# Summing the attention denominators on GpSimd in place of VectorE, in a linear-attention and MLP kernel on one core

## The chip, the cores and the metric

The kernel runs on one NeuronCore of a Trainium2 chip. The metric is the time of one execution on the device in microseconds (us), as the median of several runs. TensorE multiplies matrices, VectorE and ScalarE work elementwise and along rows, GpSimd here does reductions over partitions, and SyncE (SP) issues the transfers, one after the other in its own queue. All engines run side by side and each works its own queue in order; what has to wait for another engine waits on a semaphore.

## The reference

```python
batch, n_heads, seq, head_dim = (8, 8, 576, 64)      # d_feat = 128
def phi(x):
    proj = np.einsum('bhsd,df->bhsf', x, w_phi)
    proj = proj - np.max(np.abs(proj), axis=-1, keepdims=True)
    return np.concatenate([np.exp(proj), np.exp(-proj)], axis=-1)
q_p, k_p = (phi(q), phi(k))
kv = np.einsum('bhsf,bhsd->bhfd', k_p, v)
z = np.sum(k_p, axis=2)
num = np.einsum('bhsf,bhfd->bhsd', q_p, kv)
den = np.einsum('bhsf,bhf->bhs', q_p, z)[..., None] + 1e-06
attn = num / den
...
x = attn.transpose(0, 2, 1, 3).reshape(B * S, H * D)   # 4608 x 512
r = np.maximum(x @ w_in, 0.0)                          # d_ff = 2048
return (r * r) @ w_out
```

For each of 64 heads, a feature map of 2 x 128 exponentials is made of the queries and of the keys; `kv` and `z` collect the keys, `num` and `den` apply them to each query, and the quotient goes through a two-layer network with a squared ReLU. The change is about how `den` is formed: one number for each of the 576 queries of a head, a sum over 256 features.

## The kernel before

The 64 heads are worked in 32 pairs. A pair's tokens are 576 columns; the two heads of a pair lie on the partitions, 64 dimensions each, or 128 features each. Four pairs make a batch element, 576 tokens. The network runs over 18 chunks of 256 tokens, each in 8 blocks of 256 hidden columns: `gemm1` (24 products, line L1164), a squared ReLU on ScalarE and VectorE that yields a high part `gh` and a low part `gl`, then `gemm2` (L1195). The last four chunks take another form of the second product (L1440). A chunk can start as soon as the tokens of its pairs lie in a ring of buffers (`ring`, written by `tokens`, L937 to L959).

All of this is interleaved. Every piece of work is entered by `P.add(engine, us, function, after, buffers, rank, ...)`; a planner (`Plan.order`) runs through it like a clock, with a cost in us for each piece, one free time for each engine and the buffers that a piece holds, and takes on each engine the ready piece of the lowest rank. The order that comes out is the order of the instructions on each engine. The ranks of most pieces come from a string, `RANKS`, two characters each:

```python
op.rank = (90 * i + j - 3000) * 0.05
```

The argument `lock` stands for a resource that VectorE and GpSimd share in the planner: a GpSimd piece with a lock waits for the end of a VectorE piece with one, and such a VectorE piece is lengthened by what is left of a GpSimd piece, up to `lock` us.

Pairs 0 to 5 (`early`) run beside the loading and splitting of the weights. They form their denominators on TensorE, and `denominators` (L917) adds 1e-6, takes the reciprocal on a tile `den` of 128 x 9 (L919, L920), writes it to DRAM (`rd`), and `spread` reads it back onto all partitions (`rb`).

Pairs 6 to 31 (`visit` and `late`) go like this. In `late`, TensorE projects the queries with the features on the partitions (L1065), the result is copied to `pt` (L320, L322), GpSimd takes the maximum over partitions of each head (`partition_all_reduce`, L1088), VectorE subtracts it, ScalarE takes the two exponentials (L1093, L1095), and ScalarE and VectorE weigh them with `z` into y, which stands in `pt` (L1100, L1102): the denominators are then the sums of y over 128 partitions. VectorE forms them in steps: it transposes 32 x 32 blocks into `yt` (L1106), sums along the rows into `d4` (L1107), SP takes the result through DRAM (`dd`, then `da`) so that the four blocks of partitions come side by side, and VectorE adds them, adds 1e-6, takes the reciprocal and transposes back (`inverse`, L1117 to L1120). Two transfers write it to `rd`, and `spread` follows. `yt` has one buffer, which the sums of `z` use too (L1041, L1043); `pt` has one buffer. `narrow` (L655 on) splits queries and keys into halves with a scale that GpSimd finds by small maxima (L664).

Of the kernel before, what the change touches and what calls it, by code (L numbers as in the profile page):

```python
# [301 lines left out]
def tile_kernel(ctx, tc, qp, kp, vp, w_phi, w_in, w_out, out):  # L302
# [332 lines left out]
    def narrow_weights(rank):  # L635
# [4 lines left out]
            wk[1], wk[0], channels=128, reduce_op=bass_isa.ReduceOp.max), [o, pool_next], [], rank, lock=0.0)  # L640
# [395 lines left out]
    def late(p):  # L1036
# [48 lines left out]
        for h in range(2):  # L1085
# [20 lines left out]
            o = P.add("DVE", dve_us(S), lambda n=n, y=y: V.transpose(yt_["y", n - 2 * EARLY], y()), [o], [("pt", p), ("yt", ("y", n - 2 * EARLY))], R(RQ + 0.9))  # L1106
            dens.append(P.add("DVE", dve_us(S), lambda n=n, h=h: V.tensor_reduce(  # L1107
                out=d4_[p][:, h, :], in_=yt_["y", n - 2 * EARLY].rearrange("p (b x) -> p b x", x=32), op=ALU.add, axis=AX.X),
                [o], [("yt", ("y", n - 2 * EARLY)), ("d4", p)], R(RQ + 1.0)))
# [3 lines left out]
        o = P.add("SP", 0.4, lambda: SP.dma_start(da_[p], dd_[p].rearrange("(a x) y -> x a y", a=4)), [o],  # L1113
                  [("dd", p), ("da", p)], R(RQ + 1.1), land=1.9, xfer=0.1)

        def inverse():
            V.tensor_reduce(out=dr_[p][:, 0:36], in_=da_[p].rearrange("p a x -> p x a"), op=ALU.add, axis=AX.X)  # L1117
            V.tensor_scalar(out=dr_[p][:, 0:36], in0=dr_[p][:, 0:36], scalar1=1e-6, scalar2=None, op0=ALU.add)
            V.reciprocal(out=dq[:, :, 0:18], in_=dr_[p].rearrange("p (h x) -> p h x", h=2))
            V.transpose(dt_[p], flat(dq))  # L1120
# [4 lines left out]
        def keep():
            for h in range(2):
                SP.dma_start(rd_[p].rearrange("(h x) y -> h (x y)", h=2)[h].rearrange("(b x) -> b x", x=32),
                             dt_[p][0:18, 32 * h:32 * h + 32])
# [113 lines left out]
    def norm(src, after, rank, j, i):  # L1242

        keys = [("j", j)], [("n1", i)], [("n2", i)]
        box = lambda: j_.at(j, [128, KT, T], BF16)
# [3 lines left out]
        o = P.add("POOL", par_us(T), lambda: G.partition_all_reduce(  # L1249
            n2_[i], n1_[i], channels=128, reduce_op=bass_isa.ReduceOp.add), [o, pool_next], keys[1] + keys[2], rank, lock=0.0)  # L1250
# [318 lines left out]
    "W.if#M#F8n#L,_6.89$W/E#z--$l%x.;+i+3%z)G$5&E$V$5(j+(!|1E*y5U$L#L&V#L-111(q?,$7.m#=WxK*4.NmoDAw>*-t,E"
    "G.`$D-WD!G*(HfMKRnkkJ!&iLH&w,rS49g0+EzH5LC%Y!GK3U=1A*3a)*D1PJW1iEcopphh5T,]$_[(aQp!_$*&dK*H)6g1IvchL"  # L1570
    "-{Ty#ksC[8iCv!e[0[?lQl3G8{5^N0Ba(bT9ix,CV2leVy`0($Q8pp8!/ZdsrKQ`PERPxl#|<g(pt*3J#<3%2}xly!e^R&ynpSyW"
    "uFu.q]gkzPL;QYzQq4(5xTn`zJ2(v*Mb]iOh|b?YgwR_n-KIj5RZxPhV[sadjQW|W*oRk8wVdmA3y?o*tJ}M{TPG>.:EX-PXL6,T"
    "ClMR*t_[X41`LUI1dZ|xaV}/{?<|z-t^lRi*v6i[mW|Vz=|X}+e)r7Ax`+K,DVC,FK*/;9vj=}nQA7M6*;Vl}i^c27s$K$5pVS5P"
# [79 lines left out]
```

## Time and profile before

| | us |
|---|---|
| median of 3 runs | 1032.64 |
| lowest and highest run | 1032.29, 1034.31 |
| profiled execution | 1029.46 |
| its span, first to last instruction | 1027.7 |
| TensorE matmul busy | 994.9 |
| VectorE busy | 824.1 |
| ScalarE busy | 740.5 |
| GpSimd busy | 169.1 |

The profile is one execution. In its rows, PE is TensorE's matmuls, PEld its weight loads, DVE VectorE, ACT ScalarE, POOL GpSimd and SPq the queue of SP. A row of a group gives line, engine, operation, the tile written and the tiles read, shapes and count, then busy us and the mean in ns, then the idle time before it and what ended that. A row of a tile or a line gives the count, the shortest, median and longest duration in ns, and the first and last start in us. A row of waits says who waited for whom: us in total, times, the longest. A row of the table by stages gives the stage, its length, and for PE, PEld, DVE, ACT and POOL the busy us and the number of instructions, then the granted clock of TensorE, the share of the DMA engines and GB/s. A row of the timeline gives start, duration and what ran.

### The profile page before, as it was taken

The numbers are of one execution on the slowest core, as the hardware profiler recorded it, in microseconds if no ns is written. First come the engines' busy times: TensorE is split into PE (matmuls) and PEld (weight loads), VectorE is DVE, ScalarE is ACT, GpSimd is POOL, SyncE is SP. The second block draws the span as 40 slices with busy tenths as digits, with TensorE's granted clock in tenths as the row PEclk, the third lists the DMA queues.
The fourth block names the chain that finished last, engine by engine and source line by source line (L and its number), as shares of the span: only waits on it lengthen the run. The fifth ranks groups of instructions, "written<-read, shape, count | busy, mean of one in ns | idle before, by whom it ended". The sixth has DMA issues, their size and how long they took to land. (4 is left out here: it accounts for less than half of the span.)

```text
span 1027.7 us, 21125 instructions
## 1 busy us (share of the span) xinstructions
PE 994.9 (97%) x8247; PEld 717.0 (70%) x8310; DVE 824.1 (80%) x1547; ACT 740.5 (72%) x1346; POOL 169.1 (16%) x100
## 2 busy tenths in 40 slices
...
DMA packets 92936, 76.28 MB, mean 74 GB/s; under 512 B 61476, under 2 KB 70308, under 8 KB 90788
## 3 DMA queue, kind: packets, MB, share of 16 engines
...
## 5 line engine op out<-in xcount | busy, mean ns | idle before, releaser
L1164 PE MATMUL ph<-ring,win 128*128 128x256 f16 x3456 | 391.8, 273 | 1.4 <-DVE gl L315 1.4
L1164 PEld LDWEIGHTS <-win 128*128 128x128 f16 x3456 | 336.0, 98 | 58.5 <-issue 9.8
L1088 POOL PARTITION_ALL_REDUCE mx<-pt x52 | 116.0, 2232 | 497.7 <-ACT pt L320 196.9
L1195 PE MATMUL po<-wh,gh 128*128 128x512 f32 x456 | 146.0, 441 | 0.0
L1195 PE MATMUL po<-wl,gl 128*128 128x512 bf16 x455 | 118.2, 382 | 0.1
L1176 ACT ACTIVATE r<-ph,cw 128x512 f32<-128x512 f32 x114 | 77.6, 681 | 55.5 <-PE ph L1164 55.1
L1195 PE MATMUL po<-wl,gh 128*128 128x512 bf16 x394 | 107.0, 379 | 5.9 <-issue 3.5
L315 DVE TENSOR_TENSOR gl<-ph,gh 128x512 bf16<-128x512 f32 x114 | 77.3, 678 | 34.9 <-ACT ph L1180 31.3
L1195 PEld LDWEIGHTS po<-wh,gh 128*128 128x128 f32 x456 | 86.1, 189 | 26.2
L1195 PEld LDWEIGHTS <-gh 128*128 128x128 bf16 x456 | 42.0, 98 | 49.1 <-issue 8.2
L1195 PEld LDWEIGHTS <-gl 128*128 128x128 bf16 x456 | 35.3, 98 | 58.3 <-issue 26.7
L1178 ACT ACTIVATE gh<-r 128x512 fp32r<-128x512 f32 x114 | 71.1, 624 | 3.7 <-PE po L1195 1.5
L1180 ACT ACTIVATE ph<-r 128x512 f32<-128x512 f32 x114 | 67.0, 588 | 0.4
L768 PE MATMUL pv<-e,v 128*64 128x256 f32 x512 | 62.8, 389 | 3.2 <-ACT kz L322 2.0
L315 DVE TENSOR_TENSOR qe<-pt,mx 128x576 f32<-128x576 f32 x52 | 39.0, 751 | 20.2 <-POOL mx L1088 18.7
L315 DVE TENSOR_TENSOR v<-qe,gh 128x896 f16<-128x896 f32 x30 | 32.6, 1089 | 27.2 <-ACT gh L1428 27.0
L1093 ACT ACTIVATE qe<-qe 128x576 f32<-128x576 f32 x52 | 35.2, 677 | 20.1 <-DVE qe L315 19.8
L1102 DVE SCALAR_TENSOR_TENSOR pt<-qe,zc,pt 128x576 f32<-128x576 f32 x52 | 42.1, 809 | 9.5 <-ACT pt L1100 9.2
L768 PEld LDWEIGHTS pv<-e,v 128*64 128x64 f32 x512 | 35.0, 141 | 20.7 <-ACT kz L322 2.9
L1413 ACT ACTIVATE r<-ph,cwr 128x512 f32<-128x512 f32 x30 | 20.6, 686 | 34.2 <-PE ph L1164 34.0
L1440 PEld LDWEIGHTS <-gh 128*128 128x128 f16 x420 | 41.1, 98 | 4.8
L1249 POOL PARTITION_ALL_REDUCE n<-n x12 | 22.2, 1848 | 119.3 <-DVE n L1247 79.7
...
## 6 DMA issues: line engine op xcount, KB each, us to landing
...
kz<-td SPq DMA_DIRECT2D x104, 32.0 KB
zq<-zd SPq DMA_DIRECT2D x104, 2.0 KB
```

What stands on the lines that cost most here:

```text
L315: eng.tensor_tensor(out=out_, in0=a, in1=b_, op=ALU.subtract)
L768: PE.matmul(out=to[64 * h:64 * h + 64, 0:256], lhsT=v_[p][:, t, h, :], rhs=e_[2 * p + h][:, t].rearrange("p s f -> p (s f)"), start=t == 0 ...
L1088: o = P.add("POOL", par_us(S), lambda n=n, h=h: G.partition_all_reduce(mx_[n], pt_[p][:, h, :], channels=128, reduce_op=bass_isa.ReduceOp. ...
L1093: o = P.add("ACT", act_us(S), lambda qe=qe: A.activation(out=qe(1), in_=qe(0), func=AF.Exp, scale=-1.0), [o], [("qe", n)], R(RQ + 0.4))
L1102: o = P.add("DVE", dve_us(S), lambda h=h, qe=qe, y=y: V.scalar_tensor_tensor(out=y(), in0=qe(1), scalar=zc_[p][:, 2 * h + 1:2 * h + 2], in ...
L1164: PE.matmul(out=ph[:, j, :], lhsT=win[w][:, t, 128 * ff:128 * ff + 128], rhs=ring[half][x][:, t, c0:c0 + T], start=k == 0, stop=k == 3 * K ...
L1176: o = P.add("ACT", act_us(512, 1), lambda: A.activation(out=r_[n], in_=ph_[bank], func=AF.Relu, scale=cw[:, f, 0:1]), [g1], [("ph", bank), ...
L1178: sq = P.add("ACT", act_us(512), lambda: A.activation(out=gh_[n], in_=r_[n], func=AF.Square), [o], [("r", n), ("gh", n)], Q)
L1180: o = P.add("ACT", 0.59, lambda: A.activation(out=ph_[bank], in_=r_[n], func=AF.Square), [o], [("ph", bank), ("r", n)], Q, other=("DVE", 0 ...
L1195: PE.matmul(out=po_[po[i][1]], lhsT=g[:, j, 128 * i:128 * i + 128], rhs=w[:, j, :], start=(f == (NFP - ENDS if last else 0) and (s, j) == ...
L1249: o = P.add("POOL", par_us(T), lambda: G.partition_all_reduce(n2_[i], n1_[i], channels=128, reduce_op=bass_isa.ReduceOp.add), [o, pool_nex ...
L1440: PE.matmul(out=to, lhsT=l()[:, a], rhs=r(slice(b_, b_ + 1))[:, 0], start=(f == 0 and k == 0 and place % 2 == 0), stop=(f == NFP - 1 - END ...
```

## The change

In `late`, the transposition, the row sums, the two transfers through DRAM and the long `inverse` go. In their place GpSimd sums y over partitions for each head, by `partition_all_reduce` with `add`, into `yt`; one transfer for each head takes one row of the result into the 128 x 9 tile `den`, and the `denominators` function that pairs 0 to 5 use does the rest. All `partition_all_reduce` pieces, old and new, are entered with `lock=None`, so the planner no longer counts them for the shared resource. The tiles of the old steps go, and the string of ranks is another one, with two pieces fewer for each of the 26 pairs.

```diff
-    dd_ = tiles(dr, "dd", [128, 36], F32, 2, EARLY)
-    d4_ = tiles(sm, "d4", [128, 2, 18], F32, 1, EARLY)
-    da_ = tiles(sm, "da", [32, 4, 36], F32, 1, EARLY)
-    dr_ = tiles(sm, "dr", [32, 36], F32, 1, EARLY)
-    dt_ = tiles(sm, "dt", [32, 64], F32, 1, EARLY)
...
-    dq = cp.tile([32, 2, 32], F32, name="dq")
...
-    V.memset(dq, 0.0)
...
             o = P.add("POOL", par_us(S), lambda n=n, h=h: G.partition_all_reduce(
                 mx_[n], pt_[p][:, h, :], channels=128, reduce_op=bass_isa.ReduceOp.absmax),
-                [pt[0], pt[1 + h], pool_next], [("pt", p), ("mx", n)], R(RQ + 0.2), lock=0.0)
+                [pt[0], pt[1 + h], pool_next], [("pt", p), ("mx", n)], R(RQ + 0.2), lock=None)
...
-            o = P.add("DVE", dve_us(S), lambda n=n, y=y: V.transpose(yt_["y", n - 2 * EARLY], y()), [o], [("pt", p), ("yt", ("y", n - 2 * EARLY))], R(RQ + 0.9))
-            dens.append(P.add("DVE", dve_us(S), lambda n=n, h=h: V.tensor_reduce(
-                out=d4_[p][:, h, :], in_=yt_["y", n - 2 * EARLY].rearrange("p (b x) -> p b x", x=32), op=ALU.add, axis=AX.X),
-                [o], [("yt", ("y", n - 2 * EARLY)), ("d4", p)], R(RQ + 1.0)))
-
-        o = P.add("SP", 0.4, lambda: SP.dma_start(dd_[p], flat(d4_[p])), dens, [("d4", p), ("dd", p)], R(RQ + 1.1),
-                  land=1.9, xfer=0.1)
-        o = P.add("SP", 0.4, lambda: SP.dma_start(da_[p], dd_[p].rearrange("(a x) y -> x a y", a=4)), [o],
-                  [("dd", p), ("da", p)], R(RQ + 1.1), land=1.9, xfer=0.1)
-
-        def inverse():
-            V.tensor_reduce(out=dr_[p][:, 0:36], in_=da_[p].rearrange("p a x -> p x a"), op=ALU.add, axis=AX.X)
-            V.tensor_scalar(out=dr_[p][:, 0:36], in0=dr_[p][:, 0:36], scalar1=1e-6, scalar2=None, op0=ALU.add)
-            V.reciprocal(out=dq[:, :, 0:18], in_=dr_[p].rearrange("p (h x) -> p h x", h=2))
-            V.transpose(dt_[p], flat(dq))
...
-        o = P.add("DVE", 0.95, inverse, [o], use, R(RQ + 1.1), lock=4.0)
...
-        o = P.add("SP", 0.7, keep, [o], [("dt", p), ("rd", p)], R(RQ + 1.1), land=1.9, xfer=0.1)
...
+            key = [("yt", ("y", n))]
+            o = P.add("POOL", 3.56, lambda n=n, y=y: G.partition_all_reduce(
+                yt_["y", n], y(), channels=128, reduce_op=bass_isa.ReduceOp.add), [o], [("pt", p)] + key,
+                R(RQ + 0.9), lock=None)
+            dens.append(P.add("SP", 0.5, lambda n=n, h=h: SP.dma_start(
+                den_[p][64 * h:64 * h + 64], yt_["y", n][0:1].rearrange("j (r x) -> j r x", x=9)), [o],
+                [("den", p)] + key, R(RQ + 1.0), land=2.1, xfer=0.1))
+
+        denominators(p, dens, lambda h: rd_[p].rearrange("(h c r) x -> h c (r x)", c=2, h=2)[h].unsqueeze(0).to_broadcast(
+            [64, 2, SH]), R(RQ + 1.1))
...
-    "2{E!VZ&L$^O6(*5%-iV(D=6%E}8(1QS^iie/I`Tah!BjSAa18U7u838rvqGxgEVBwm84DII)w9[Xrvy!LR.sT%|Eg=vlGX{6mA0E"
...
+    "C^D[FxBfEXD^D6F*DhCDI3DGGEEEG`I@GWH?GUH-FBHEGxH>HNHNG{HGEuIoFnM)HXHNGjH(GsGtHKI1DVISFvI<HXIJJ)HnIEHd"
...
```

More of the change, by code (lines that the diff above doesn't have):

```diff
@@ L639, in narrow_weights @@
         o = P.add("POOL", par_us(1), lambda: G.partition_all_reduce(
[L640 removed]
+            wk[1], wk[0], channels=128, reduce_op=bass_isa.ReduceOp.max), [o, pool_next], [], rank, lock=None)
         def bits():
@@ L664, in bound @@
             G.partition_all_reduce(x[:, 0:2], ka_[p], channels=128, reduce_op=bass_isa.ReduceOp.max)
-        o = P.add("POOL", par_us(2), bound, last + [pool_next], uses[:2], rank + 0.1, lock=0.0)
+        o = P.add("POOL", par_us(2), bound, last + [pool_next], uses[:2], rank + 0.1, lock=None)
         def bits():
@@ L1122, in late @@
-        use = [("da", p), ("dr", p), ("dt", p)]
-        o = P.add("DVE", 0.95, inverse, [o], use, R(RQ + 1.1), lock=4.0)
[L1125 to L1128, printed above, removed]
-        o = P.add("SP", 0.7, keep, [o], [("dt", p), ("rd", p)], R(RQ + 1.1), land=1.9, xfer=0.1)
-        spread(p, o, lambda h: rd_[p].rearrange("(h c r) x -> h c (r x)", c=2, h=2)[h].unsqueeze(0).to_broadcast([64, 2, SH]),
-               R(RQ + 1.1))
+            key = [("yt", ("y", n))]
@@ L1249, in norm @@
         o = P.add("POOL", par_us(T), lambda: G.partition_all_reduce(
-            n2_[i], n1_[i], channels=128, reduce_op=bass_isa.ReduceOp.add), [o, pool_next], keys[1] + keys[2], rank, lock=0.0)
+            n2_[i], n1_[i], channels=128, reduce_op=bass_isa.ReduceOp.add), [o, pool_next], keys[1] + keys[2], rank, lock=None)
         return o, i, keys[2]
@@ L1274, in split_norms @@
         o = P.add("POOL", par_us(NFP), lambda: G.partition_all_reduce(
-            wt[:, NFP:], wt[:, 0:NFP], channels=128, reduce_op=bass_isa.ReduceOp.max), rows + [pool_next], [], rank + 5.0, lock=0.0)
+            wt[:, NFP:], wt[:, 0:NFP], channels=128, reduce_op=bass_isa.ReduceOp.max), rows + [pool_next], [], rank + 5.0, lock=None)
         def bits():
@@ L1569 @@
[L1569 to L1573, printed above, removed]
@@ new lines @@
+    "HkIRHdH0HtH}JWIPILH|HaJ;I>I-ITJ6HoM9K(E@IBEyL7FTICHxERK=P4INI#IAI7J3EVHZM%JZI#J%JoHWJ,K%JGJhJgJfLrEG"
+    "K5N&L$KKMIL%J_L%LWLSOgNULLN*H,ItJ$PLK@IYN(K}KlInJAJEGrJAJ2IVIMR(Q&I}GeQOJyPrQ;O/ChM^O!GgMxP#I>N}O%PB"
+    "NqN8RzNzBvCHD$DJD,?GD{MnDRCsD;D#CADMDKC^DYDcDiAJD`DbCzD,D}D.D2D;D4DTCQDNDmDcD0F3D&F/HHF0DrC[F>G7HRE6"
+    "CaB/CxDIDSDaE>E<DxDjE=HdBcE8F[?HG_G*FMD;E+F2GpEcC<E!GcE(E^EqE;HOF%I)E`E^DaB2BOBWAbCA@|HxC7D^Cl?`BVAB"
+    "EkByBPBbBPBL@(BiBF;FAaDVC$@}AHE*;JF)C{Ee?IA|Bb?QC4E!@&B{BLB=AM@bBv@WBOITFQG^EYG|FeGmJ)G%G7G?KXK`>wB4"
@@ new lines @@
+    "EDG?FdG%FbF%GOG7G:DZG^GVGsE|GTIJFhGfFMH[<XGdHrFeG9FyG6E<GEC0F>L2H9J9E!J=I$H]HOH_F;D^K0D@FXErGkH=H_J5"
+    "H]BaN&H@I9I^J4GgErGiH8JXI!I&H$GNF0I$F5I>HGEjK{KJGtLnF*JzI1JbIJCNIOJ!I-HBHtMNI:IHJ)EgJ=KzG7FVIfJUH^K5"
+    "FmG]I/IqIdJ$HoH&HJIrJ2J1DyMNJgJoL|NNFnJZP-GsG3F!J7J/ImI#IyIyM%I3I.I6K%I6E:IOJZJYJNIrGeK^KXL.KBOVNtJI"
+    "L;McL=LlMYI,J%MKGUITIHKcMBC|GWIRJZJYJBHDJKJKM=KTK>K$@,JEJ$J`J*JYJyMpK[I^M)IXJxK[LMF,P.IbL8PfKqO+HyKZ"
+    "KLS7I1FHLHHJJ)I}J<JpKzLSM!KTMrMXKOP}LHP!L!GPGjK|NZKuQtSyN6N0JhGhOBHvFQO?QHCxK/K4OeHyKpK.PPDDLoFhJiHL"
@@ new lines @@
+    "LGOpRDJYG5CyNhF[NlR&JgN/GVM+FRI6MyM3JLG^MRKvGvKZNrE?QjJAKZO`AXD)K6VnIzIRN1GmNXQ*CwMyT_LlNrO?R5N|M<G2"
+    "R!S!G!JYM&O]FYOnJ(OdO_JiS-UpTGRfJRH[QZTzQWPGOiRBPnQQUvRLLDKAMdR,McO{L?F=N3MtJcKLPCU2Q;JGO$J8P|OOMv]2"
+    "MeL$JPKKT8KOK8RtJlN4NCPFK[O,RzPTNNT!QpL!NcQEQZUcOgO:QVRIOoO7LuQ{OJPYRDR{NlSGPbPvPqWGR^P_NSR=T<M9PZSV"
+    "TyR9M1O1T1TiT`PG`!PlO]LUT]ORSdMzY:O=Q!KUPZM*RyP@Q/PIQ4OjPoQ!Q=PGPWL%ImTeDFPIPkOaNnO3SCQMNUSIHfPOS!SE"
+    "OsT)P&O0NoOHH@N#JeNhQ6IWMTLCTHNpP6W5R(LNOBN.SDMQM2VuREPXOuN=TORNQ!ODPsIGL@N-Q`O/JUQjQRPKREQ.NKTMQXLr"
@@ new lines @@
+    "K4KuOqKZQhT;PkPuWVT9Q(RbOWO]MELjN{QAQ[SnN&RoOANZPLN#S.M2MWPRQ+UHLwRAS9OxKEN?KtPNOeOAUmPCRRQWP0SURFLi"
+    "S*QHL%NAQDN;JuO;L{Q(O=UBPmTtPoNxQTTdQkUTX)T-W4UoUBP2Q)StSpQwQ%PyTJQ>R8SOOvR#ShQSSIQ+PuR8UrQOWaN}PGK#"
+    "R1SiNqafYFUrWjWdZ^UJQ-Y5K}X7P7OTKKR>WPLoO.VUS=TLRGR9UFTjR:UFUsRoRQYTSrOMMrHwKpMzLcPEK>MuPxJ;M6IhOtQ["
+    "KnPTHBI]IaS$QCODP^NzN`JjPVOMAsNJJpL9Q/P0PdNALTP6QUV|TTNdNZG$LNVmLbQIN^O_U)O|QOJ/P5PWOfJ3N_Q:JKLlO:Th"
+    "VBXmT=UfQ,UkJoTFTzWNR6RVOLV&UCP7W0NmPvU6RLSmRLT,VyW8PsRhRAOxLCO[Q=S4R.V+U}K{T{VRZ3R}Uf^9X=Pj^EPqWiV."
@@ new lines @@
+    "U1Z^P`XKVkRaR>SaSbRoRrT!]1`jOUQRTnR9T6RVQyRXM@Q(RWSZR#S?Q6V]L]R*SRR&QVU]R9QFT%QoQ>ONSPYrT&SqP>P0UBSg"
+    "R*PoPjNpSPMyTGQ6U!M/K@MkS7SpR6QiWES)QIP}QlYqQKS(V{WfWmY;[*Y;WX_aN@S%Q-T;R1TLUFS{S}R`WQZEX[`4]v]pZYXy"
+    "W3V^]CX`S7].VT^)Yn_VYIVrUQXYX,XzVJWRY-SmXXTLY-U}SD[[X|]qV,UGV5_z`D^jW8b9X9V(Q.Y0YkWn_[b2^lYiYuZXXla%"
+    "`h_8a+^BXVYo]oV[U1THT5XRWiTmYkKwUXVIS]U/R)`[U1U9V^Z/W.W:W.VmW|V&QlX#YYXwV&_QX6W{];XuXSU0VQTZX%X[YsTT"
+    "ZSWoS,POXpXtZQUe[fW2YVXtWfXZWfZ1WpXKZ!XMX8Y3VhVhWWXvXtZSU=YDS3V@W#V_V,TfTXWoW!YuSXUiZBYKX(Z;UOXoW+]0"
@@ new lines @@
+    "ZIQ_Y-Z^Ws`*Zj`_UXWOX=Vk]xWLWUZ*UyV,[$RV]eW8]+].Y8f?[lX)_T[pZeW3`)U`UeXnX_ToU]T6XuWBTrVyXeTiVZWOYjV>"
+    "XvW0ZLV0XdXTWuUuW_X-ZLU3Y=V+XZY@RjP9ZSS+Y2We[i[eVyXyVVXKRvU}YaWrS7S]Z-W-VDR}XCXBS^UGRu_<X+ShYYYCYgXb"
+    "VF[&ZfZ9W!W7X-UjUPXuU7W?S>XxZ5VjWg[k[>Y]PwY&]R[tY/ZWZxWxYX[QWP_E^BY$_MZyZ2^2ZZ]ZX3]4[kXdVnZ6Yg]Z[)]g"
+    "W8Z$VAY][4ZdYl]A]GRq]{Yw]oYhW$dj[1Zs_vZQYr[D]2W|[zZ=^#]DZ7UpWFTuXUZH]hU_Z,ZfUwZvYK]0]dXN^>YUWbY{Ut[+"
+    "Y@X8XHX!ZYU&Z,V2WQZgQWScY?QKZ8VmZcX(Ys[)VeY,V_OQXUUOWOWfXKX:VtYhbk^6Z4[sTnV]Y4YfY5_KU?]k^`X1ZkUuS;X]"
@@ new lines @@
+    "SbYGX._+Z8^hY>ZANZSpW4Q|R)W7S_ZBW2_i^$[UbfW]V7RU[0Mh[RXVS1YB[>c_W>Q3W%N3TTW=bNU[X)^=O(UeUXV$W|X&V?a7"
+    "XtV&U.ZXSwVyUgXX_yWJRHZrUPVS_E]A`&[}YrVYbGYyWz[Z`t[=^!Z6^jYoc8[-`{^bXCU[[HY_SIWK^]]>Y:[XVx[)`p^vZ>dt"
+    "^y[__([cfw`.[]aucmZ>X{`xeFe-d|YMfHcEg`ZZV`VmZ-]waxfhYAX}YK^oZu^2Xn]D`qSoZI_&Y0awZ&^OZdadXvg3^5Z6U>aV"
+    "YA_9]LV4[6ULYbX5a-XiT}Xac/U|X+d=ZvZ^daTic7Y{Yec/]`_b]U^pdVZ5`YUtX<T6bigQfN_c`wT$Y7[LZNc.^]d|^<T&XH_q"
+    "dx[C`^es^k]hXPZx_#[rZoWnZ`V<bt]QZ_[QZ&WHWC_:_z]R`FcY^4]f]2]+X?`!al`V^w_t[i_jc0a+]R[eW![!^V[ObF_a[yZp"
@@ new lines @@
+    "^MZh_^cpaa][X{aO[VY}VJ_!b=^1YYWQU{^N^r_Nf>d&`k_/]$`z_.[cZ_a+]F^V`k`*]=^]a]_T`we/^Q`tfEb1a;d?a``?^ZiC"
+    "]o_)bW_X`P_t]t`*`h`Gcvd@e$b1^e_pbB_l^edxcjehak`_^h]xgxaVcEa)Y_ZH^s__b<cCb%exfVbFbS`W_F_TcbckaUa<_ZZE"
+    "]`^2_Xa^c]cHdb`FcggTfSZ;`]d3aT]R_1[YbX[Zece^cOdS]e[<b{bEbTcHfcg0YchjcqXpcsf6hz`8Xob-aQfzoGdPdZ^=]J[x"
+    "aAYodrb}lNc<_5mbc/c;`vbH`lVmc^et_TboYScx[]dUapb5`$aFd7e,`@^>`M]p`ia_c9^BdEc%ah_-bvfH`;fUd*[6`t`,c:a="
+    "`_dx`c^ler]-ZncNgu_J_?cU_x_r[kdHa[fya}ZV_jedesd^ckiNddbs^P_r^F`?_vaVcJbNgi[7dTbZcx[pb$abaY^/bC`?cC]W"
@@ new lines @@
+    "d+avbhbo`eaIn4dea[a.a%_:bia#b+a7gv_yd)a{c>_0fYdgdsZ#au^YZRh!].c-d/`J`Ba=[Qa[f1bcfkaD`cd.c*hZ`ob%c%e:"
+    "b@e<a`gTdVb;f@bzc^iEbVb^bqe-ae^gb<cdbQb2ayeDeIa._Ze8e4bBdjbcf^c^`#c^b-g)c2ece}hOas_d_>eeeidnb/g<cqm6"
+    "_gbmcPkaamj.dCg}cHc|bQa(^^b7c]a?[!X!^{fma;di]4aXg^guitba_ldY_/jGf`g8jP`{`ddtb?cwaJj<iDe3dMg:d@]KhGdL"
+    "elem^UWy]@fta/eWYdZ4ag`*ZiZ4_8`s[u]y]{fL^e`$_KUJaV[n^g`K_-`Fa8^8al[la)aNe4[>ZMZc]e`z_vd._;FwRiOQL@K="
+    "NyVoR-TuQzMtOeO#Q&NyR-PST]Q*M_QtP9RHX&R_VWPaPQG[QFNqPON8L7L_UCElS+SoSoV2[FS:VJTkRYOuQ[PHIMP%PTP#ViT("
```

57 lines of the change are left out of this document (8 added, 49 removed).

## The prediction

> **What bounds the kernel now.** I read the page's totals first, then the table by stages, then the waits of TensorE in the two parts that the table separates.
>
> ```profile
> span 1027.7 us, 21125 instructions
> PE 994.9 (97%) x8247; PEld 717.0 (70%) x8310; DVE 824.1 (80%) x1547; ACT 740.5 (72%) x1346; POOL 169.1 (16%) x100
> ...
> 0.00:125.00 125.00, 103.19 (x1068) 71.43 (x1071) 108.27 (x173) 108.61 (x189) 17.55 (x12) 0.97 0.58 208
> 125.00:875.00 750.00, 742.98 (x5845) 514.37 (x5905) 626.66 (x1200) 553.34 (x1022) 147.92 (x86) 1.00 0.25 64
> ```
>
> The span is 1027.7 us and the profiled execution took 1029.46, so 1.76 lie around the span. The median of the runs is 1032.64: 3.2 above the profiled execution. I sum against 1029.46 and add 3.2 at the end.
>
> The stage table is the argument. Of 1027.7 - 994.9 = 32.8 idle us of TensorE, 125.0 - 103.19 = 21.8 lie in the first stage, 750.0 - 742.98 = 7.0 in the long middle and so 4.0 after it. Pairs 6 to 31 live in the middle: their first GpSimd maximum starts at 145.4 us and their last at 829.1 (row below). So the change is made in the stage where TensorE has 7 us to give back, and VectorE, although 84% busy there (626.66 of 750), is not what TensorE waits for:
>
> ```profile
> PE po L1195 <- issue: 3.5, 22, 0.2
> PE pn L418 <- ACT pt L322: 0.8, 1, 0.8
> PE pp L1065 <- DVE e L731: 0.3, 1, 0.3
> PE po L1195 <- ACT r L1176: 0.2, 1, 0.2
> ...
> PE po L703 <- DMA k<-in_kp_dram: 4.4, 1, 4.4
> ```
>
> The first four lines are all the waits of TensorE from 125 us on: 3.5 us is its own issue, and only 0.3 us of the 4.8 was spent behind VectorE. The last is the longest of the first 125 us, a load, which the change leaves as it is.
>
> **The change part by part.**
>
> ```profile
> L1106 DVE STREAM_TRANSPOSE yt<-pt x52: 735/769/780, 155.5 to 837.6; 128x576 f32<-128x576 f32 x52
> L1107 DVE TENSOR_REDUCE d<-yt 128x18 f32<-128x576 f32 x52 | 38.5, 741 | 0.4
> L1117 DVE TENSOR_REDUCE dr<-da 32x36 f32<-32x144 f32 x26 | 10.0, 386 | 9.3 <-DMA da<-dd 9.3
> L1118 DVE TENSOR_SCALAR dr<-dr 32x36 f32<-32x36 f32 x26 | 8.5, 327 | 0.9
> L1119 DVE RECIPROCAL dq<-dr 32x36 f32<-32x36 f32 x26 | 9.5, 367 | 0.9
> L1120 DVE STREAM_TRANSPOSE dt<-dq x26: 232/232/236, 172.7 to 846.6; 32x64 f32<-32x64 f32 x26
> L919 DVE TENSOR_SCALAR den<-den x6: 154/164/483, 40.1 to 160.2; 128x9 f32<-128x9 f32 x6
> L920 DVE RECIPROCAL rc<-den x6: 215/216/217, 40.3 to 160.4; 128x9 f32<-128x9 f32 x6
> ```
>
> *Removed from VectorE.* The two large steps give 52 x 0.769 = 40.0 and 38.5, 78.5 us; the inverse of each pair gives 10.0 + 8.5 + 9.5 and 26 x 0.232 = 6.0, 34.0 together. *Added:* 26 short inverses in the form that pairs 0 to 5 use, 26 x (0.164 + 0.216) = 9.9. Net -102.6: 824.1 would be 721.5. Worth to TensorE: by the waits above, at most the 0.3 us behind VectorE, and never more than the 7.0 idle in that stage. I take 0. The cover is the other way round here: it is TensorE's own queue of work that hides VectorE, so relief of VectorE is not time.
>
> *Added to GpSimd.*
>
> ```profile
> L664 POOL PARTITION_ALL_REDUCE kb<-ka x20: 365/376/826, 245.3 to 784.1; - x20
> L1088 POOL PARTITION_ALL_REDUCE mx<-pt x52: 2140/2142/2674, 145.4 to 829.1; - x52
> L1249 POOL PARTITION_ALL_REDUCE n<-n x12: 1793/1794/2437, 604.7 to 919.5; - x12
> ```
>
> No sum over 576 elements is in the trace. A maximum over 2 elements took 0.38 us (median), one over 576 took 2.14 (median); a sum over 256 took 1.79. From the sum's row: (1.79 - 0.38) / 254 = 5.6 ns an element, so 0.38 + 574 x 0.0056 = 3.57 us for 576. The ends: 1.79 + 320 x 3.1 ns (the maximum's slope, (2.14 - 0.38) / 574) = 2.8 and 576/256 x 1.79 = 4.0. I take 3.57, since it is from the same operation, and it adds 52 x 3.57 = 186 us: 169 becomes 355 of 1027.7, so GpSimd is still idle two thirds of the time.
>
> *What a sum does to VectorE while it runs.* This is the cost that the order no longer knows: the planner's locks for these operations are taken out.
>
> ```profile
> 617.01 1.79 POOL L1249 PARTITION_ALL_REDUCE n<-n  x1 [3.25 <-DVE wn L1260]
> 617.16 0.97 DVE L670 TENSOR_SCALAR kb<-kb 128x2 f32<-128x2 f32 x1
> 428.44 2.53 POOL L1088 PARTITION_ALL_REDUCE mx<-pt  x1 [14.04 <-ACT pt L320]
> 429.00 1.41 DVE L759 TENSOR_TENSOR es<-es,et 64x256 f32<-64x256 f32 x1
> L759 DVE TENSOR_TENSOR es<-es,et x52: 394/420/1409, 127.7 to 803.2; 64x256 f32<-64x256 f32 x52
> ```
>
> At 617.16 VectorE began a scaling of 2 elements behind a sum that had begun at 617.01. By the row of the inverse of pairs 0 to 5, a scaling as small takes 0.164 us (median); here it took 0.97 and ended at 618.13, 0.67 before the sum did: the sum held it for the first 618.13 - 0.16 - 617.01 = 0.96 of its 1.79 us. At 429.00 an addition whose median is 0.42 took 1.41 within a maximum that ended at 430.97 and by its normal length had begun at 428.83; it was let go near 430.0, 1.17 of 2.14 us. Both are about 0.54 of the operation (0.96 / 1.79 and 1.17 / 2.14), so a sum of 3.57 us would hold 1.93. If every one of 52 sums held VectorE for all of that: 52 x 1.93 = 100 us, and VectorE is at 721.5 + 100 = 822, where it was. The other end is nothing, if only reductions and PSUM readers run beside the sums. No row shows how often, so I take the middle, 50 us, which enters no sum: at 772, and at both ends too, VectorE's total cannot become the bound.
>
> The Trainium skill, page "SBUF — State Buffer", section "Who interferes with whom", says that the loser of the pair of ports that VectorE and GpSimd share "fully blocks" for the whole instruction. By that rule the 52 sums would hold 52 x 3.57 = 186 us; the 0.96 of 1.79 us above speaks for a hold of about half, so I price the full hold only as a rival below.
>
> *What is late.* The single hold matters more than the sum of them: one VectorE result up to 1.9 us later than the order assumes.
>
> ```profile
> 679.22 0.68 DVE L315 TENSOR_TENSOR gl<-ph,gh 128x512 bf16<-128x512 f32 x1
> 681.30 0.55 PEld L1195 LDWEIGHTS <-gl 128*128 128x128 bf16 x4 [0.28 <-issue]
> ```
>
> The result gl ended at 679.22 + 0.68 = 679.90 and TensorE loaded it at 681.30: 1.4 us in hand, less than one hold. Such thin places exist, then, in an order that did know the locks; the new order is made as if a sum or a maximum cost VectorE nothing, so it has no reason to keep holds away from them. Bounds: 0 if every hold falls where more is in hand; 52 x 1.93 = 100 if every sum stops TensorE for all of its hold. Of the two the trace is far nearer to 0: 0.3 us of waits behind VectorE against 2.1 us for the two holds above. I take one hold in twenty of the 104 (52 sums, 52 maxima, whose holds of 1.17 us were planned for and now are not): 104 / 20 x about 1 us = 5 us.
>
> *The path of one pair.* From the second half's y to the inverse it was 0.77 + 0.74, two DMA hops and 0.386 + 0.327 + 0.367 + 0.232; it becomes one sum, one hop and 0.38.
>
> ```profile
> L910 SPq DMA_DIRECT2D den<-sx x6: 575/586/707, 30.4 to 156.5; - x6
> SPq L1113 <- DMA dd<-d: 19.5, 18, 2.0
> L937 DVE TENSOR_TENSOR rb<-n,rb x32: 709/750/1722, 48.6 to 855.5; 128x576 f32<-128x576 f32 x32
> ```
>
> A hop is an issue (0.59 for the den row, which the new transfers take after) and a landing; SP waited at most 2.0 us for dd to land. So 1.51 + 2 x 2.4 + 1.31 = 7.6 before, 3.57 + 2.6 + 0.38 = 6.6 after: no loss. Behind a sum in GpSimd's queue stand the next maxima and the small maxima of L664, up to 3.57 us late, and behind those the subtraction of VectorE and the scalings of ScalarE; with GpSimd idle two thirds of the time the order has room between them. SP issues four transfers a pair up to rd now (dd, da, two rd) and three after (two den, one rd), so the loads queued behind it in SP's order are not worse off, except that the wait in front of them is for a sum and no longer for VectorE.
>
> *Buffers.* The sum holds yt until the den transfer has left, and holds pt in place of the transposition. From the copy of the projection on, with rows of this trace: three copies 0.73 + 0.49 + 0.49, maximum 2.14, subtraction 0.75, two exponentials 1.35, scaling 0.76, addition 0.81: the first y is there after 7.5 us; its sum and transfer end at 7.5 + 3.6 + 2.6 = 13.7, and the second sum at 17.3. Pairs follow each other at (829.1 - 145.4) / 51 x 2 = 26.8 us, so the path fits, with 9 us to spare where it had 14.
>
> ```profile
> L315 DVE TENSOR_TENSOR qe<-pt,mx x52: 704/751/1051, 149.5 to 831.2; 128x576 f32<-128x576 f32 x52
> L1093 ACT ACTIVATE qe<-qe 128x576 f32<-128x576 f32 x52 | 35.2, 677 | 20.1 <-DVE qe L315 19.8
> L1095 ACT ACTIVATE qe<-qe 128x576 f32<-128x576 f32 x52 | 35.2, 676 | 0.7
> L1100 ACT ACTIVATE pt<-qe,zc x52: 757/764/778, 152.7 to 835.1; 128x576 f32<-128x576 f32 x52
> L1102 DVE SCALAR_TENSOR_TENSOR pt<-qe,zc,pt x52: 774/809/820, 153.5 to 836.1; 128x576 f32<-128x576 f32 x52
> L320 ACT ACTIVATE pt<-pp,sc x19: 719/723/741, 298.3 to 824.8; 128x576 f32<-128x576 f32 x19
> L320 ACT ACTIVATE pt<-pv,sc x19: 482/488/503, 299.6 to 825.8; 128x288 f32<-128x288 f32 x19
> ```
>
> *The order found anew.* In the quoted string the old sort keys run from -149 to 254 and the new ones from -40 to 243, worked out by the decoding line in `improve`. Nothing of before shows what it does. Inside the middle it can win no more than 7.0 us. In the first 125 us, 21.8 us are idle, 4.4 of them before the first load lands, so 17 can move: with VectorE (108.27 of 125) and ScalarE (108.61) both near 87% busy on fixed work, half of it, 8 us, is the most that I allow for a gain, and the same for a loss. I take 0.
>
> **Sum.** 1029.46 + 0 (relief) + 5 (holds) + 0 (path, buffers) + 0 (order) = 1034.5, and + 3.2 = 1037.7, say 1037.5 for the median: slower by 0.5%.
>
> **The rivals.**
>
> 1. *Hidden anyway: no change.* The holds fall where results have many us in hand, as nearly all do now, and both orders fill TensorE. Then 1029.46 + 0 + 3.2 = 1032.7, with 2 us either way (0.2%, about what a measurement of this kernel can tell from no change). For it: 0.3 us of waits behind VectorE. Against: two different orders agreeing to 2 us.
>
> 2. *Faster, by the first stage.* The new order fills 4 to 10 of the 17 movable idle us of the first 125 us and the holds cost 0 to 2: about 1026. It needs VectorE and ScalarE above 92% in that stage. Against it: no operation that the change removes runs before 155.5 us, where the first transposition stands (row L1106 above). It decides when the idle time there falls under 17 us.
>
> 3. *The pair's path becomes the pace.* If holds and waits for the one yt stretch the path from 17.3 beyond 26.8 us, each us more puts 26 us on the attention part. The last product with the spread inverse starts at 855.5 now (row L937); three chunks of eight blocks depend on it. A block is 24 products of the first kind, 23.58 / 216 = 0.109 us each by the row below, and 21 of the second, which I take at the same: 4.9 us, 118 for 24 blocks. Of the 172 us that are left, some 45 can so be lost unseen, allowing 9 for the ends, or 1.7 us a pair. At 2.5 us too much: 26 x 2.5 - 45 = 20 us, 1053. Against: 9 us to spare.
>
> ```profile
> 868.46 23.58 PE ph L1164 x216
> ```
>
> 4. *Full holds.* With 186 us held, VectorE is at 721.5 + 186 = 908, and in the middle at 626.7 - 102.6 + 186 = 710 of 750. Nearly full, it would make TensorE wait for perhaps a third of the 40 us that are left: 1046. The trace's 0.54 speaks against it. It is the rule of the page named above, taken word for word.
>
> **How the numbers follow.** Holds not planned for, as summed (1035 to 1044): 37%. No change (1030.6 to 1034.7): 28%. Faster (1020 to 1030.5): 25%. The pair's path: 6%; full holds: 4%. Slower by over 0.2% is 37 + 6 + 4 = 47%. The likeliest alone is 1035 to 1044. The range leaves out the lower end of the faster case and the two dear rivals' upper ends: 1022 to 1047.
>
> **What would show it.** Right: VectorE's count falls by 208 - 52 = 156 instructions (eight a pair go, two come) and one clearing, GpSimd's rises by 52 with sums of 3.57 us, additions like L759 reach over 2 us beside a sum, and TensorE's idle time between 125 and 875 us rises from 7.0 to about 12, put down to VectorE. Wrong: sums far from 3.57 us; idle time in the middle still 7; or the first stage's 21.8 us moved by more than 4, which would make the result a matter of the order and not of the sums.

## The result and the profile after

The changed kernel takes 1065.89 us (median of 6 runs), the kernel before 1032.64: slower, ratio 1.031 with a 95% interval of 1.029 to 1.033. 33 us were lost where 5 were forecast. The profiled execution of the changed kernel took 1065.27.

The page of the changed kernel, totals and two of the rows in 40 slices:

```profile
span 1063.5 us, 21048 instructions
PE 1006.0 (95%) x8248; PEld 721.8 (68%) x8310; DVE 795.7 (75%) x1393; ACT 734.7 (69%) x1343; POOL 362.3 (34%) x152
DVE  6988897866587774776877679987788769984553
POOL 0020134544543435423445346654354450110000
```

VectorE's share falls from 80% to 75% and GpSimd's rises from 16% to 34%; TensorE, which nothing was taken from or given to, has a lower share of a longer span. The table by stages (length, then busy us of PE, PEld, DVE, ACT, POOL, the clock, DMA) says where:

```profile
0.00:125.00 125.00, 104.16 (x1062) 71.53 (x1065) 102.60 (x172) 104.13 (x183) 16.21 (x12) 0.97 0.60 212
125.00:875.00 750.00, 717.29 (x5605) 493.82 (x5662) 566.92 (x984) 526.25 (x980) 336.93 (x137) 0.99 0.23 61
875.00:1000.00 125.00, 124.89 (x1064) 105.16 (x1064) 98.78 (x190) 77.88 (x138) 9.17 (x4) 1.00 0.05 16
1000.00:1063.50 63.50, 59.68 (x522) 51.33 (x520) 27.37 (x49) 26.43 (x44) 0.00 (x0) 0.99 0.05 18
```

The first 125 us are as before: 125 - 104.16 = 20.8 us idle, 21.8 before. The middle has 750 - 717.29 = 32.7 us of idle TensorE in place of 7.0. Of 35.8 us more span, 25.7 lie here as plain idle time. (Both profiles lack some matmul records, 63 before and 62 now of the 8310 that other profiles below show, so both idle times may be a little too large; their difference is hardly touched by it.) The waits of TensorE in that stage:

```profile
PE ph L1138 <- DVE gl L315: 13.0, 11, 1.9
PE pp L691 <- DVE k L677: 8.0, 6, 2.6
PE pp L1058 <- DVE e L724: 3.6, 4, 2.4
PE po L1169 <- issue: 2.9, 18, 0.2
PE pp L691 <- ACT k L673: 2.4, 2, 2.0
PE po L1169 <- DVE o L1187: 1.1, 2, 0.7
PE ph L1138 <- DVE ring L952: 0.7, 1, 0.7
PE ph L1138 <- DVE ring L956: 0.2, 1, 0.2
```

Six of the eight lines end in a result of VectorE: 13.0 + 8.0 + 3.6 + 1.1 + 0.7 + 0.2 = 26.6 us, against 0.3 us before. One such wait in order of time; start, duration, engine, and in brackets the idle time before and what ended it:

```profile
820.96 3.59 POOL L1100 PARTITION_ALL_REDUCE yt<-pt  x1 [2.12 <-DVE pt L1095]
821.27 2.83 DVE L677 SCALAR_TENSOR_TENSOR k<-k,kb,k 128x576 f16<-128x576 f32 x1 [0.40 <-ACT k L673]
...
824.16 0.40 PE L691 MATMUL pp<-whigh,k 64*128 64x128 f16 x4 [2.58 <-DVE k L677]
```

The sum starts at 820.96. At 821.27 VectorE starts to split the next pair's keys (L677), which has two inputs in SBUF; its median is 0.82 us, here it took 2.83 and ended at 824.10. TensorE, which needs these keys for its next products, started at 824.16 after 2.58 us of nothing. Taking 0.82 off its end, VectorE was let go near 823.3, 2.3 us into a sum of 3.59. Other cases come out alike; two of them:

```profile
734.39 3.59 POOL L1100 PARTITION_ALL_REDUCE yt<-pt  x1 [1.60 <-DVE zc L1048]
734.65 2.88 DVE L677 SCALAR_TENSOR_TENSOR k<-k,kb,k 128x576 f16<-128x576 f32 x1 [0.26 <-ACT k L673]
...
641.50 3.59 POOL L1100 PARTITION_ALL_REDUCE yt<-pt  x1 [1.72 <-DVE pt L1095]
641.96 2.09 DVE L663 TENSOR_SCALAR kb<-kb 128x2 f32<-128x2 f32 x1
```

The first was let go 734.65 + 2.88 - 0.82 - 734.39 = 2.3 us into its sum, and a scaling of two elements, which otherwise takes some 0.16, at 641.96 + 2.09 - 0.16 - 641.50 = 2.4 us.

And the price is not only the wait. The same place in stages of 5 us, with an earlier one for comparison (PE busy is the first number after the length, PEclk the third from the end):

```profile
800.00:805.00 5.00, 2.42 (x24) 1.54 (x23) 3.75 (x10) 2.60 (x6) 0.00 (x0) 1.00 0.18 40
805.00:810.00 5.00, 5.00 (x39) 3.84 (x38) 2.84 (x5) 5.00 (x10) 0.09 (x1) 1.00 0.31 73
...
820.00:825.00 5.00, 1.99 (x26) 1.15 (x26) 4.60 (x5) 3.52 (x6) 3.59 (x1) 0.81 0.08 3
825.00:830.00 5.00, 5.00 (x36) 2.84 (x34) 0.52 (x2) 0.00 (x0) 3.46 (x1) 0.50 0.01 0
```

With 3.0 us idle between 820 and 825, TensorE's granted clock fell to half, and it is busy from 825 to 830 at 0.50 of the clock. It does not follow every wait: 2.6 us idle between 800 and 805, 2.4 of them in one wait, left it at 1.00. Over the span the granted clock was 0.990, before 0.997; 0.010 x 1063.5 - 0.003 x 1027.7 = 7.5 us. Idle time (24.7 us more in all, 57.5 against 32.8) and clock together are 32.2 of the 35.8 us; the other 3.6 are not accounted for. The clock's part changes from one execution to the next: over the six of the changed kernel it was 0.989 to 0.997, and the one at 0.997, the clock of the profile before, still had a span of 1058.2 us, 30.5 above that profile's. So most of the loss needs no lower clock.

The Trainium skill, page "TensorE: Matmul & The Clock Gate", section "Part 1: The HAM clock gate", has the clock at half after an idle window of some 3.4 us. The trace agrees in kind; here less than 2.58 us in one piece were enough, since within that wait, from 823 to 824, the clock was at 0.57 already:

```profile
823.00:824.00 1.00, 0.00 (x0) 0.00 (x0) 1.00 (x1) 0.52 (x1) 1.00 (x1) 0.57 0.08 2
```

### The profile page after: what moved, and what is told of

It is laid out like the page before. It is cut to its first block, busy times and chain, and to the rows that moved or that the text cites. A ratio compares the mean times of both kernels' runs of the same rounds, so it can differ in the third digit from the quotient of the medians.

```text
span 1063.5 us, 21048 instructions
## 1 busy us (share of the span) xinstructions
PE 1006.0 (95%) x8248; PEld 721.8 (68%) x8310; DVE 795.7 (75%) x1393; ACT 734.7 (69%) x1343; POOL 362.3 (34%) x152
## 4 chain that ended last, share of the span: by engine, by line
PE 52%; DVE 21%; ACT 10%; DMA 9%; issue 4%; POOL 2%; SPq 1%; DVEq 0%; POOLq 0%; ACTq 0%
PE ph L1138 21%; PE po L1169 14%; PE pv L761 3%; PE pp L1414 2%; PE po L1414 2%; DMA k<-in_kp_dram 2%; DVE gl L315 2%; DMA rb<-rd 2%; DVE k L677 2%; PE pn L982 2%; PE pn L1414 1%; DVE qe L315 1%; DVE ring L952 1%; DVE n L1221 1%; DVE rb L930 1%
## 5 line engine op out<-in xcount | busy, mean ns | idle before, releaser
L1138 PEld LDWEIGHTS <-win 128*128 128x128 f16 x3456 | 335.8, 98 | 73.4 <-issue 26.6
L1100 POOL PARTITION_ALL_REDUCE yt<-pt x52 | 191.1, 3676 | 144.1 <-DVE pt L1095 74.7
L761 PE MATMUL pv<-e,v 128*64 128x256 f32 x512 | 68.2, 411 | 1.2 <-ACT e L729 1.0
L315 POOL TENSOR_TENSOR wl<-u,wh 128x1024 bf16<-128x1024 f32 x8 | 20.3, 2535 | 119.0 <-ACT wh L517 94.3
L761 PEld LDWEIGHTS pv<-e,v 128*64 128x64 f32 x512 | 37.5, 147 | 19.3 <-issue 3.4
```

What stands on the lines that cost most here:

```text
L315: eng.tensor_tensor(out=out_, in0=a, in1=b_, op=ALU.subtract)
L761: PE.matmul(out=to[64 * h:64 * h + 64, 0:256], lhsT=v_[p][:, t, h, :], rhs=e_[2 * p + h][:, t].rearrange("p s f -> p (s f)"), start=t == 0 ...
L1100: o = P.add("POOL", 3.56, lambda n=n, y=y: G.partition_all_reduce(yt_["y", n], y(), channels=128, reduce_op=bass_isa.ReduceOp.add), [o], [ ...
L1138: PE.matmul(out=ph[:, j, :], lhsT=win[w][:, t, 128 * ff:128 * ff + 128], rhs=ring[half][x][:, t, c0:c0 + T], start=k == 0, stop=k == 3 * K ...
```

## The experiments

Two theories could explain more waits behind VectorE. A: the sums hold VectorE, and the order does not know it. B: the new order is poor by itself, whatever the sums do. Later runs split A further.

**The sums cut short, in the same order.**

```diff
...
+            def total(n=n, y=y):
+                for _ in range(1):
+                    G.memset(yt_["y", n], 2.5e14)
+                G.partition_all_reduce(yt_["y", n][:, 0:64], y()[:, 0:64], channels=128, reduce_op=bass_isa.ReduceOp.add)
...
```

> The changed kernel, with each sum over partitions cut to 64 of its 576 columns, behind one fill of the tile (the other denominators are then a constant, so the output is not the reference's); the order of all instructions is that of the changed kernel. A sum should take some 0.4 + 64 x 0.0056 = 0.8 us and the fill about 0.5, in place of 3.68. Theory A (the sums hold VectorE longer than the order assumes, and TensorE waits for the late results): the 44 us that VectorE lost beside the sums shrink to under 10, TensorE's idle time from 125 to 875 us falls from 32.7 to 8 to 15, and the time to 1035 to 1045. Theory B (the new order is poor by itself, whatever the sums do): the time stays at 1055 to 1068.

Measured: 1039.97 us, ratio to the kernel before 1.006 (1.004 to 1.009). Without the sums' length, 26 of the 33 us are gone. Theory B can hold for the other 7 at most.

**GpSimd as busy as in the changed kernel, but hardly reading.** The loop of fills runs five times.

> As the kernel with the sums cut to 64 columns, but with five fills of the tile ahead of each sum, so that GpSimd is busy for about as long as the full sum (five times some 0.55 us and 0.8, 3.5 us) while it reads almost nothing from SBUF (the output is again not the reference's); same order. Theory A1 (what costs is that VectorE is held beside the sum): 1035 to 1045, about as with the short sums. Theory A2 (what costs is GpSimd's time itself: denominators, the next maxima and the transfers queued behind them come late): 1055 to 1068, with VectorE hardly lengthened beside the sums.

Measured: 1043.39 us, ratio 1.010 (1.007 to 1.014). The page of this kernel, its sums and fills on GpSimd, and the sums of the changed kernel (busy us, mean ns):

```profile
PE 1001.1 (96%) x8248; PEld 720.5 (69%) x8310; DVE 751.0 (72%) x1393; ACT 734.3 (71%) x1343; POOL 359.7 (35%) x412
```

```profile
L1102 POOL MEMSET yt<- 128x576 f32 x260 | 152.3, 586 | 93.6 <-DMA den<-yt 53.2 <-DVE z L1036 28.4
L1103 POOL PARTITION_ALL_REDUCE yt<-pt x52 | 39.2, 755 | 14.9 <-DVE pt L1095 10.6 <-POOL yt L1102 0.2
...
L1100 POOL PARTITION_ALL_REDUCE yt<-pt x52 | 191.1, 3676 | 144.1 <-DVE pt L1095 74.7 <-DMA den<-yt 40.5 <-DVE z L1036 21.6
```

A sum takes 5 x 0.586 + 0.755 = 3.69 us on the mean here, 3.68 in the changed kernel, and GpSimd is busy for 359.7 us, 362.3 there. VectorE issues the same 1393 instructions in both, and is busy for 751.0 us here and 795.7 there: the 44.7 us between them I take as VectorE held beside the sums, 0.86 us for each of 52. Taking the hold away and leaving the order and GpSimd's time brings 1065.9 to 1043.4: 22.5 us. So every second us of hold reached TensorE. The 3.4 us between this kernel and the one with short sums are GpSimd's time. Theory A1's range is met and A2's is not.

**The old sums in the new order.** All pieces that both kernels have keep the new ranks; the pieces of the old sums have ranks of their own around those of the new ones.

> The kernel before, with VectorE's transposes and sums, under the changed kernel's order: the planner without locks for GpSimd's reductions and the new ranks for all pieces that both kernels have; the pieces of the old sums got ranks of their own around those of the new ones. In the planner's terms it ends at 1029.5, the changed kernel at 1029.4. Theory A (the sums' holds cost the time): 1033 to 1042, since only the maxima, some 1.2 us each, still hold VectorE unplanned. Theory B (the new order is poor by itself): 1055 to 1068.

Measured: 1039.74 us, ratio 1.006 (1.003 to 1.009). The new order costs 6 to 7 us with the old sums as well, and it is the same amount that the short sums left over. Its stages:

```profile
0.00:125.00 125.00, 105.27 (x1056) 72.05 (x1059) 100.77 (x170) 102.73 (x180) 16.19 (x12) 0.96 0.60 211
125.00:875.00 750.00, 735.42 (x5774) 508.24 (x5826) 628.77 (x1182) 546.46 (x1017) 146.25 (x85) 1.00 0.24 63
```

**The holds made known to the planner, and the ranks searched on.**

```diff
-                locked[e] = op.end
+                locked[e] = op.end - (lock * us if e == "POOL" else 0.0)
...
-        o = P.add("DVE", 0.53, bits, [o, whole_of["w"]], uses[1:], rank + 0.1)
+        o = P.add("DVE", 0.53, bits, [o, whole_of["w"]], uses[1:], rank + 0.1, lock=4.0)
...
-                R(RQ + 0.9), lock=None)
+                R(RQ + 0.9), lock=0.38)
```

and `lock=0.38` likewise for the other reductions over partitions.

> The sums on GpSimd as in the changed kernel, but the planner knows that GpSimd's reductions hold VectorE, for the first 62% of their time as the changed kernel's trace shows it (and that the small scaling of the narrow step is held too), and the ranks were searched on under that planner, from the changed kernel's ranks; the computation is the same. In the planner's terms it ends at 1036.6. Theory A (the time was lost because the order did not know the holds): 1034 to 1043, with TensorE idle 8 to 18 us between 125 and 875 us in place of 32.7. Theory C (the holds cost about as much whatever the order does, for VectorE has no room left around them): 1050 to 1066.

Measured: 1047.90 us, ratio 1.013 (1.011 to 1.016). Theory A's range was missed by 5 us at its upper end, but 18 of the 33 us come back with the same sums. Its stages, its totals and one row of TensorE's waits, from the fastest of its five executions (1043.96):

```profile
0.00:125.00 125.00, 101.79 (x1054) 67.50 (x1056) 103.00 (x170) 104.04 (x182) 16.23 (x12) 0.97 0.58 210
125.00:875.00 750.00, 743.69 (x5848) 512.12 (x5845) 579.22 (x1008) 544.72 (x1010) 339.71 (x137) 1.00 0.24 62
875.00:1000.00 125.00, 120.63 (x1089) 107.08 (x1088) 87.60 (x177) 72.55 (x128) 5.38 (x3) 0.99 0.04 13
```

```profile
PE 1004.6 (96%) x8310; PEld 718.9 (69%) x8310; DVE 790.2 (76%) x1389; ACT 738.9 (71%) x1347; POOL 361.3 (35%) x152
```

```profile
PE ph L1138 <- DVE ring L952: 2.7, 1, 2.7
```

VectorE is held about as much as in the changed kernel: it is busy for 790.2 us, 795.7 there, of instructions that differ by four. But TensorE idles 6.3 us in the middle, about as little as before the change (7.0 with 60 matmul records missing there). Planned for, the holds fall where nobody waits. The ranks were searched on as well as the holds made known, and no run has the longer search alone, so the 18 us belong to the two together. What is left lies elsewhere: 23.2 us idle in the first stage and 4.4 between 875 and 1000, 2.7 of them in one wait for the last pairs' tokens (`ring`).

**The same treatment for the old sums.** Planner with the holds, the same search from the new ranks.

> VectorE's transposes and sums as before, with the planner that knows the maxima's holds for 62% of their time, and ranks searched on in the same way and for as long as for the sums on GpSimd with their holds planned (that one took 1047.9). In the planner's terms it ends at 1029.4, 7.3 before that one. Theory A with its corollary (the 6 us that the old sums lost in the new order came from the maxima's holds, which that order did not know): 1029 to 1035, so by 0 to 0.4% at most the best of all. Theory B' (orders found by this search are worse on the chip by themselves): 1037 to 1045.

Measured: 1031.65 us, ratio 0.998 (0.9964 to 0.9996). Theory B falls for orders of this search as such: with the holds known, they run as well as the old one; 0.2% better is at the edge of what the interval can tell. The same treatment that gave the sums on GpSimd 18 us gave the old sums 8. That the new order's 6 to 7 us with the old sums were what it did not know of the maxima is not shown: the two kernels differ in the locks and in all ranks. The profile of the old sums in the new order, with its 14.6 us idle in the middle, speaks against it. The longest wait there, 1.7 us at 127, comes before the first maximum at 156.6. Of the ten longest, none has an operation of VectorE lengthened by over 0.3 us beside a maximum in the 15 us before it. The stages of the kernel with the old sums and the holds planned:

```profile
0.00:125.00 125.00, 107.05 (x1064) 72.72 (x1065) 103.38 (x173) 104.49 (x183) 17.25 (x12) 0.96 0.60 212
125.00:875.00 750.00, 745.27 (x5880) 513.10 (x5880) 631.27 (x1187) 553.96 (x1025) 148.60 (x85) 1.00 0.24 63
```

Beside the 1047.90 above it is also the fairest comparison here of the two ways to sum: both planned, both searched alike, the sums on GpSimd come out 16 us behind. The planner said 7.3. Not all of it need be the sums': between the two profiled executions lie 11.2 us, and 5.3 of them are idle time of TensorE in the first 125 us, while the first sum on GpSimd starts at 163.6.

**Each sum in four parts, in the changed kernel's order.**

```diff
...
+                for x in range(0, S, 144):
+                    G.partition_all_reduce(yt_["y", n][:, x:x + 144], y()[:, x:x + 144], channels=128,
+                                           reduce_op=bass_isa.ReduceOp.add)
...
```

> The changed kernel in its own order, with each sum over 576 columns made as four sums over 144, one after the other. By 0.4 us for each plus 5.6 ns an element a sum takes four times 1.2, 4.8 us in place of 3.68, and a single hold some 0.7 us in place of 2.3. Theory A3 (the length of one hold is what reaches TensorE: VectorE slips in between two parts): 1040 to 1052, with no operation of VectorE lengthened by over 1.5 us. Theory A4 (the holds' total is what counts): four holds of 0.7 are 2.8 us a sum, more than 2.3, so the time is 1062 to 1080.

Measured: 1076.68 us, ratio 1.042 (1.039 to 1.045). By the time, theory A4; by the profile, of the slowest of its five executions (1081.73), neither:

```profile
PE 1018.4 (94%) x8310; PEld 725.1 (67%) x8310; DVE 764.0 (71%) x1393; ACT 734.4 (68%) x1343; POOL 420.4 (39%) x308
```

```profile
DVE den L912 <- DMA den<-yt: 37.6, 19, 7.0
```

```profile
L1102 POOL PARTITION_ALL_REDUCE yt<-pt x208 | 250.5, 1276 | 136.0 <-DVE pt L1095 69.4 <-DMA den<-yt 32.6 <-DVE z L1036 18.9
```

VectorE is busy for 764.0 us, 32 less than in the changed kernel, so the holds' total did not grow. But a sum takes 4 x 1.276 = 5.1 us, and VectorE stood 37.6 us in front of the short inverse until `den` had landed; in the changed kernel it was 8.6:

```profile
DVE den L912 <- DMA den<-yt: 8.6, 9, 2.0
```

VectorE takes its queue in order, so what stands behind the inverse comes late too. That would be a second way from GpSimd to TensorE, without any hold.

**GpSimd busy that long, hardly reading.** Seven fills.

> The kernel with the sums cut to 64 columns and fills ahead of them, with seven fills in place of five: GpSimd is busy for 7 x 0.59 + 0.76 = 4.9 us a sum, as long as with the sums in four parts (5.1), and reads as little from SBUF as with five fills (the output is not the reference's); same order. Theory A5 (what made the sums in four parts so slow was their length of 5.1 us against the 3.56 that the order counts on: VectorE stands in its queue at the short inverse until den has landed, 37.6 us in all there): 1060 to 1075, with VectorE's waits for den over 25 us. Theory A4 (the holds' total made them slow): 1043 to 1050, since there are no holds.

Measured: 1060.39 us, ratio 1.027 (1.024 to 1.029). Two more fills, 1.17 us a sum, cost 17 us, and the wait is the same one; the totals and the row of this kernel,

```profile
PE 1008.5 (95%) x8310; PEld 721.0 (68%) x8310; DVE 750.5 (71%) x1393; ACT 735.1 (69%) x1343; POOL 422.4 (40%) x516
...
DVE den L912 <- DMA den<-yt: 33.5, 18, 5.3
```

and of the kernel with five fills

```profile
DVE den L912 <- DMA den<-yt: 4.7, 4, 1.9
```

Theory A5 holds. With five fills a sum takes 3.69 us, with the planner's 3.56 nearly met, and little waits; at 4.9 and 5.1 the denominators come after VectorE has got to them. So the length of the sum beyond what the order counts on costs as well as the hold. The sums in four parts take another 16 us with nearly the same length; VectorE is busy for 764.0 us there and 750.5 here, so holds are part of it, but these 16 us were not taken apart. In the changed kernel, where the sum's length is nearly as planned, VectorE waits 8.6 us in all for `den`, and the step from short sums to five fills puts the cost of GpSimd's time at 3.4 us.

## Why the prediction was wrong

The sign and the place were right: slower, in the middle, through VectorE's results, with the first stage unmoved (20.8 us idle against 21.8, forecast 0). The size was not: 1065.9 lies outside 1022 to 1047.

- *Relief of VectorE worth nothing:* it held. In the same new order, VectorE is busy for 748.9 us with the short sums and for 831.2 with the old ones, and the times are 1039.97 and 1039.74.
- *The sum's length:* forecast 3.57, measured 3.59 (median of the rows below). *The hold:* forecast 0.54 of it, 1.93 us. Measured: 2.3 of 3.59 in the rows at 820.96 and 734.39, so 0.65. The most that one operation lost, by the last row below, is 2.497 - 0.152 = 2.35 us. Mis-sized by a fifth: the share of 0.54 had been read beside a sum over 256 columns and a maximum, and it is not the same for a sum over 576.

```profile
L1100 POOL PARTITION_ALL_REDUCE yt<-pt x52: 3592/3593/4094, 166.0 to 874.6; - x52
L677 DVE SCALAR_TENSOR_TENSOR k<-k,kb,k x20: 776/819/3084, 280.9 to 821.3; 128x576 f16<-128x576 f32 x20
L592 DVE TENSOR_SCALAR cc<-cb x13: 128/152/2497, 20.9 to 622.7; 128x4 f32<-128x4 f32 x6, 64x1 f32<-64x1 f32 x6, 128x9 f32<-128x9 f32 x1
```

- *All holds together:* forecast between 0 and 100 us with 50 taken, measured 44.7. Near, but by luck: 50 was the middle of a range, taken because no row showed how often a hold falls on work. VectorE's total came to 795.7 all the same, not 772: without these holds it is 751.0 and not 721.5. What makes up the difference, the maxima's holds or pieces that the order gave it in ScalarE's place, was not taken apart. The counts came as forecast for GpSimd (152, 52 more) and nearly so for VectorE (1393, 154 fewer; forecast 157).
- *How many of them reach TensorE* is the step that failed, the term "one hold in twenty", 5 us. It was to cover sums and maxima alike; the kernel with five fills puts the sums alone at 22.5 us, half of all their hold. I took the figure from how rarely TensorE waited for VectorE in the kernel before. But those 0.3 us were not a property of VectorE's work: the order had been found under a planner that kept the holds away from thin places. With the holds planned and the ranks searched on, the same sums leave TensorE 6.3 us idle in the middle; unplanned, 32.7. (The 3.5 us that I read as TensorE's own issue seem to be missing records: the profiles here with all 8310 matmuls have no such row.) A quiet trace of an order that knows a cost says nothing about an order that does not.
- *The order found anew:* forecast 0; 6 to 7 us with the old sums. Rightly bounded at 8, but it lay in the middle (14.6 us idle against 7.0) and not in the first stage (19.7 against 21.8), where I had allowed for it. Why is open.
- *The clock* was no term at all: the stretch after 820 us shows one such case, and by the mean clocks it comes to 7.5 us over the span of the profiled execution, but to less in others.
- *Rivals:* full holds (4%) were half wrong in the mechanism, since 0.65 of a sum holds, and with 1046 still 20 us short. That VectorE's total would fill up is not what happened: it was at 566.92 of 750 us in the middle when TensorE waited for it most. The pair's path as the pace did not come about. The den wait, a late GpSimd result in front of VectorE's queue, I named only as room that the order would have; GpSimd's time costs 3.4 us here and 17 when the sum grows by 1.2 us.

The Trainium skill's sentence that the loser "fully blocks" for the whole instruction ("SBUF — State Buffer", "Who interferes with whom") would be a hold of 3.59 us, further from the measured 2.3 than the 1.93 forecast: VectorE was let go with a third of the sum to run. Its other rule there, that VectorE's two-input operations meet only a GpSimd operation that reads SBUF, agrees with the fills: GpSimd as busy, VectorE 44.7 us less.

Open: why the sums with their holds planned come out 16 us behind on the chip and 7.3 in the planner. Of the 11.2 us between the profiled executions the stages put 5.3 in the first 125 us, 4.4 from 875 to 1000 and 1.6 in the middle; whether a longer search would close it was not tried.
